# Half-array projection of 24 pairs' queries, routing kept in a PSUM bank, the next expert's sums on GpSimd, and new orders

## The chip, the cores and the metric

The kernel runs on one core of one Trainium2 chip. The core has a matrix engine (TensorE, called PE in the profile; its weight loads are the row PEld), three elementwise engines (VectorE = DVE, ScalarE = ACT, GpSimd = POOL), DMA queues (one of them issued by SyncE, called SP), an on-chip memory SBUF with 128 partitions, and PSUM, which here is one tile `ps` of eight banks of 128 x 512 float32 into which PE writes its products. Each engine works through its own list of instructions in order; semaphores hold an instruction until what it needs is there.

The metric is the device time of one execution in microseconds, the median over runs. Before the change it is 1009.02 us (1009.04, 1009.02 and 1008.69).

## What is computed

A linear attention with a feature map, whose output feeds a mixture of eight experts with a Sinkhorn routing:

```python
# q, k, v: (8, 8, 576, 64); w_phi: (64, 128)
def phi(x):
    proj = np.einsum('bhsd,df->bhsf', x, w_phi)
    proj = proj - np.max(np.abs(proj), axis=-1, keepdims=True)
    return np.concatenate([np.exp(proj), np.exp(-proj)], axis=-1)
q_p, k_p = (phi(q), phi(k))
kv = np.einsum('bhsf,bhsd->bhfd', k_p, v)
z = np.sum(k_p, axis=2)
num = np.einsum('bhsf,bhfd->bhsd', q_p, kv)
den = np.einsum('bhsf,bhf->bhs', q_p, z)[..., None] + 1e-06
x = (num / den).transpose(0, 2, 1, 3).reshape(4608, 512)

# w_gate: (512, 8); w1: (8, 512, 1024); w2: (8, 1024, 512)
logits = x @ w_gate
P = np.exp(logits - logits.max())
for _ in range(8):
    P /= P.sum(1, keepdims=True) + 1e-09
    P /= P.sum(0, keepdims=True) + 1e-09
    P *= N / E
for e in range(E):
    out += P[:, e:e + 1] * (np.maximum(x @ w1[e], 0.0) @ w2[e])
```

## The kernel before

**How the work is written down.** The program does not issue instructions directly. Each step calls `pe`, `act`, `dve`, `pool` or `dma`, which hand an operation with its reads, writes and buffers to a `Plan`. The plan sorts all of them into one order with its own estimates of durations: of the operations that could start first it takes the one written earliest, and with it the PSUM banks and buffers that this needs. So the place of a step in the text is a wish, and the lists on the engines come from the plan. Its estimates are not used as times here.

**Attention.** The 8 batches x 8 heads are 32 pairs of heads. A pair's row number is `NP * b + pr` (4 pairs to a batch), so rows 8 to 31 are the batches 2 to 7. The order of the steps is a string `order`, one letter a step, each letter taking its next pair: `a` projects a pair's k to features (tokens on the partitions), `q` projects its q in the same way to find each token's largest absolute score, `p` projects q once more with features on the partitions and takes the exponentials, `b` multiplies the k features with v, `n` and `m` multiply the q features with that for the two heads, `c` transposes the result into `xT` (the mixture's input, kept in SBUF), `r` and `g` treat the 64 tokens over and the gate, and `u` and `d` are pieces of expert 0, which needs no routing: an up piece (8 products of 512 columns and two evictions on ACT) or a down piece (8 products of 512 columns and one eviction, on ACT for odd `ts`, on DVE for even ones). The 24 `u` and 20 `d` in the string are filler for PE.

**The projection of q.** A pair's q lies transposed in `qkT`, head 0 on partitions 0 to 63 and head 1 on 64 to 127. `wphi2` holds the weights twice on a diagonal of zeros, so that a product over all 128 partitions keeps the heads apart. `tokens` (line 632) runs 4 products of 256 columns for step `q`, and `feature_rows` (line 651) 2 products of 512 columns for step `p`. Half of every such product is multiplied with zeros. Each step takes two PSUM banks: `q` gives its two back after the two maxima on DVE (line 614), `p` after the four exponentials on ACT (line 618).

**Between attention and expert 1.** After the last gate, `routing` (line 1146) runs eight rounds on DVE over `L` (128 x 36 x 8, float32): a product with the columns' factors, the row sums, their reciprocal, a product with them, the column sums over a transposed view, two subtractions that split the sums into three bfloat16 parts, one product on PE with `colw` (all ones) that adds them over the partitions, a reduction and a reciprocal. In the meantime PE runs the rest of expert 0 (`fill`, 12 up pieces and 16 down pieces). The operation `swap` (its key is `late`) gives the attention's memory to the experts' tiles when the attention's last reader is done; behind it POOL's queue loads expert 1's weights into `wx`.

**Experts 1 to 7.** The products of an expert are made with a seven-product scheme on quarters: `sums_x` and `sums_up` (lines 1434 and 1242) form sums and differences of quarters of `xT` and of `w1`, each through `sub` (line 1236), all on DVE; the first products of expert 1 (`up7`, line 1481 of the helper `wide`) need those of the first two groups of tokens and of `w1`. `sums_up` of expert 1 also waits for the routing's result `P`. From expert 2 on some of the products are split once more (`up49`, line 1613). Down products run on line 1472 and are added to the output in `acc` by DVE (line 1866) or by ACT and POOL (lines 1878 and 1881). The order of the up and down products of a unit of work is written in the table `UNITS`, one row a unit.

Of the kernel before, what the change touches and what calls it, by code (L numbers as in the profile page):

```python
# [349 lines left out]
def kernel(  # L350
# [22 lines left out]
    NG = 9  # L373
# [15 lines left out]
    colw = const.tile([128, 128], BF16, name="colw")  # L389
# [13 lines left out]
    wphi2f = wphi2.rearrange("p a b -> p (a b)")  # L403

# [31 lines left out]
    TI, GR, KM, QM, PM, NM, RM = 0, 0, 0, 0, 0, 0, 0  # L436
# [59 lines left out]
    ring("s_p", [128, NT], FP32, "rr", 1)  # L496
    ring("s_p", [128, 3, E], FP32, "cs", 1)
    ring("s_p", [128, E], FP32, "c_bc", 1)
# [243 lines left out]
    def pair_a(b, pr, t):  # L742

        h0 = (2 * pr) % 4
        s = {}
# [264 lines left out]
    def down0(g, part):  # L1010
# [5 lines left out]
        for i, ts in enumerate(tss):  # L1016
            if ts % 2:
# [37 lines left out]
    dve(128, lambda: nc.vector.memset(colw, 1.0), w=["colw"])  # L1055
# [34 lines left out]
    def stage_g(b):  # L1090
# [12 lines left out]
        "lraeaepqbwlqaqawwabwmqlltnrbppnwqbppmrmanbqaqmwwacmpnpbccpwbtcnmqnaqbclupunm"  # L1103
        "taumquglcapalbcpnqqdcenmucugbblnapmrcqdutabnqpmunpbambccddnqplanmqmducpblttb"
        "augnaqlnrbdcampcadmqeutunqcppmdcaqtdqabpbbmlrqtdnpmuaqualbnagnacctbmqulupran"
        "tdpmtdqcmdnpdabdancpcabbqmpumqbcdgnappqunburqcbugmmnqdcdanumupqbnucmcpnmbddp"
        "bqmpncncubncmmgccg"
# [34 lines left out]
    def table(buf):  # L1142

        return buf().bitcast(FP32)[:, 0:NT * E].rearrange("p (a b) -> p a b", a=NT)

    def routing():
        c_bc = None
        for it in range(8):
            rr, wv, cs, pc = new("rr"), new("T"), new("cs"), new("PP")
            lk = [("L", g) for g in range(NG)]  # L1150
            if c_bc is None:
                def u():
                    return L
                uk = lk
            else:
                ub = new("T")
                uk = [ub]

                def u(ub=ub):
                    return table(ub)  # L1160
                dve(366, lambda u=u, c=c_bc: nc.vector.tensor_tensor(
                    out=u(), in0=L, in1=c()[:, None, :].to_broadcast([128, NT, E]),
                    op=ALU.mult), lk + [c_bc], uk, shared=True)
# [901 lines left out]
```

## Time and profile before

| What | Value |
|---|---|
| median of the runs | 1009.02 us |
| span of the profiled execution, first to last instruction | 1007.1 us |
| PE busy, PEld busy | 993.4 us, 728.2 us |
| DVE, ACT, POOL busy | 897.1 us, 813.2 us, 447.0 us |
| attention, by the last transposition on PE | 0 to 203 us |
| routing on DVE | 205 to 242 us |
| first product of expert 1 | 244.2 us |
| granted TensorE clock | 1.000 of full speed |

The page of the profile gives for the profiled execution its span alone; the runs' median lies 1.9 us above it. A PE product is shown with its length through the pipeline, and products overlap, so that a busy PE need not be one at its peak; how fast PE can issue is read from long runs of equal products without a gap. A row of the view by groups reads: line, engine, operation, out<-in, shape, count | busy us, mean ns of one | idle us of the engine before them and what ended it.

### The profile page before, as it was taken

How to read it: one execution, taken by the hardware profiler on the slowest of the kernel's cores; microseconds unless marked ns; L12 is line 12 of the kernel's file. 1: busy time of each engine (PE TensorE's matmuls, PEld its weight loads, DVE VectorE, ACT ScalarE, POOL GpSimd, SP SyncE). 2: the span in 40 equal slices, each digit the busy share in tenths (PEclk: the TensorE clock that was granted, in tenths of full speed). 3: DMA queues.
4: the chain of work that ended last, by engine and by line, in shares of the span. 5: the costliest groups of instructions: out<-in, count | busy, mean ns of one | idle time of the engine just before them, and what ended most of it. 6: DMA issues, size and time to landing. Idle time of an engine off the chain costs nothing.

```text
span 1007.1 us, 23304 instructions
## 1 busy us (share of the span) xinstructions
PE 993.4 (99%) x8376; PEld 728.2 (72%) x8376; DVE 897.1 (89%) x1999; ACT 813.2 (81%) x1930; POOL 447.0 (44%) x514
## 2 busy tenths in 40 slices
PE   7899999999999999999999999999999999999998
PEld 5666666644566877777777877787778777787775
DVE  7999998987898898899989898989889988989886
ACT  7999999835979788878878788778887888778884
POOL 5778674400133344434444444444443444344443
PEclk9999999999999999999999999999999999999999
DMA  9999999181136423282327133632246222724653
GB/s 253 190 194 171 166 152 145 38 170 56 53 119 148 145 97 98 84 186 96 112 97 166 46 100 127 135 127 99 97 119 176 97 98 84 148 79 143 206 177 126
DMA packets 129748, 128.86 MB, mean 128 GB/s; under 512 B 55776, under 2 KB 98272, under 8 KB 129632
## 3 DMA queue, kind: packets, MB, share of 16 engines
q1 hardware_dynamic: 97680, 103.33, 35.5%
q0 software_dynamic: 31648, 23.86, 17.4%
q8 instruction: 65, 1.06, 0.4%
q14 instruction: 51, 0.42, 0.1%
q10 hardware_dynamic: 304, 0.20, 0.1%
HBM read 122.50 MB, written 19.53 MB: 141 GB/s over the span
## 4 chain that ended last, share of the span: by engine, by line
PE 92%; ACT 3%; DVE 2%; DMA 2%; issue 1%; POOL 0%; SPq 0%; DVEq 0%
PE ps L1472 42%; PE ps L1481 21%; PE ps L622 15%; PE ps L1613 11%; PE ps L905 2%; DMA xp<-xT 1%; ACT k L618 1%; ACT q L618 1%; DMA xi<-X 1%; PE ps L752 0%; DVE m L614 0%; ACT wx L618 0%; DVE wx L614 0%; DMA acc<-in_k_dram 0%; PE ps L934 0%
## 5 line engine op out<-in xcount | busy, mean ns | idle before, releaser
L1881 POOL TENSOR_TENSOR acc<-acc,hx 128x512 f32<-128x512 f32 x186 | 235.1, 1271 | 403.4 <-ACT hx L1878 138.5
L1472 PEld LDWEIGHTS <-hs 128*128 128x128 bf16 x1984 | 194.1, 98 | 46.6 <-issue 0.2
L1878 ACT ACTIVATE hx<-ps,P 128x256 f32<-128x256 f32 x372 | 159.3, 484 | 53.3 <-PE ps L1472 51.9
L1866 DVE SCALAR_TENSOR_TENSOR acc<-ps,P,acc 128x256 f32<-128x256 f32 x372 | 162.0, 477 | 29.8 <-PE ps L1472 28.1
L1481 PE MATMUL ps<-xT,T 128*128 128x512 bf16 x608 | 170.7, 379 | 0.0
L1472 PEld LDWEIGHTS <-hx 128*128 128x128 bf16 x1488 | 145.6, 98 | 25.1
L1472 PE MATMUL ps<-hx,hs 128*128 128x256 bf16 x992 | 144.3, 273 | 0.0
L1682 DVE CUSTOM_DVE_ANT_0 hs<-ps,U 128x512 bf16<-128x512 f32 x192 | 124.7, 684 | 10.9 <-PE ps L1481 6.6
L1613 PE MATMUL ps<-xT 128*128 128x256 bf16 x576 | 125.4, 272 | 0.0
L1481 PEld LDWEIGHTS <-T 128*128 128x128 bf16 x672 | 65.7, 98 | 40.4
L1688 ACT ACTIVATE hs<-ps 128x512 bf16<-128x512 f32 x96 | 55.8, 598 | 41.1 <-PE ps L1481 39.7
L1472 PE MATMUL ps<-wx,hs 128*128 128x256 bf16 x560 | 78.5, 273 | 0.0
L622 PE MATMUL ps<-w,hx 128*128 128x512 bf16 x288 | 73.0, 379 | 0.0
L622 PE MATMUL ps<-xT,w 128*128 128x512 bf16 x288 | 72.9, 379 | 0.0
L1472 PE MATMUL ps<-wx,hx 128*128 128x256 bf16 x496 | 72.6, 273 | 0.0
L1682 DVE CUSTOM_DVE_ANT_0 hs<-ps,X 128x512 bf16<-128x512 f32 x96 | 65.1, 683 | 7.4 <-PE ps L1613 6.6
L1472 PE MATMUL ps<-hx 128*128 128x256 bf16 x496 | 71.2, 273 | 0.0
L1613 PEld LDWEIGHTS <-xT 128*128 128x128 bf16 x576 | 56.3, 98 | 17.4
L614 DVE TENSOR_REDUCE m<-ps 128x4 f32<-128x512 f32 x88 | 58.8, 680 | 4.2 <-PE ps L622 2.0
L1472 PE MATMUL ps<-w,hx 128*128 128x256 bf16 x432 | 62.2, 273 | 0.0
L1678 ACT COPY X<-ps 128x512 f32<-128x512 f32 x96 | 58.6, 611 | 2.5 <-DVE ps L1656 2.4
L1472 PE MATMUL ps<-w,hs 128*128 128x256 bf16 x432 | 60.2, 273 | 0.0
(174 smaller groups left out, 2256.4 us busy)
## 6 DMA issues: line engine op xcount, KB each, us to landing
xT<-xi SPq DMA_DIRECT2D x48, 448.0 KB, 4.3
xT<-xd SPq DMA_DIRECT2D x72, 256.0 KB, 3.9
wx<-in_moe_w_dram POOLq DMA_DIRECT2D x8, 1024.0 KB, 11.0
v_m<-in_v_dram SPq DMA_DIRECT2D x15, 512.0 KB, 5.0
out_dram<-acc SPq DMA_DIRECT2D x14, 512.0 KB, 2.9
w<-in_moe_w_dram POOLq DMA_DIRECT2D x6, 1024.0 KB, 11.0
xT<-xp SPq DMA_DIRECT2D x24, 256.0 KB, 2.7
qk<-in_k_dram POOLq DMA_DIRECT2D x12, 256.0 KB, 5.2
```

The costliest lines, as they stand in the source:

```text
L614: dve(el, lambda: nc.vector.tensor_reduce(out=dst(), in_=src(), axis=AX.X, op=ALU.max, apply_absolute_value=True), r, w)
L618: act(el, lambda: nc.scalar.activation(out=dst(), in_=src(), func=ACT.Exp, bias=0.0, scale=scale), r, w)
L622: nc.tensor.matmul(out_, lhsT=lhsT, rhs=rhs, start=start, stop=stop)
L1472: pe(256, lambda i=i, k=k, z=z: nc.tensor.matmul(bank()[:, 256 * i:256 * i + 256], lhsT=lhs(k, i), rhs=rhs(k), start=first and z, stop=k = ...
L1481: pe(512, lambda k=k: nc.tensor.matmul(bank().rearrange("p (a b) -> p a b", a=2), lhsT=lhs(k), rhs=rhs(k), start=first and k == 0, stop=k ...
L1613: pe(256, lambda: nc.tensor.matmul(halves_of(bank[q], n)(), lhsT=lhs(), rhs=t()[:, rhs, :], start=start, stop=True, skip_group_check=True) ...
L1678: act(512, lambda: nc.scalar.copy(out=flat(to[q])(), in_=bank[q]()), [bank[q]], [(to[q], 0), (to[q], 1)])
L1682: dve(515, lambda: nc.vector._custom_dve(ADD_SAT, out=out_(q, i, j), in0=bank[q]().rearrange("p (a b) -> p a b", a=2), in1=to[q](), s0=3.0 ...
L1688: act(512, lambda: nc.scalar.activation(out=out_(q, i, j), in_=bank[q]().rearrange("p (a b) -> p a b", a=2), func=ACT.Relu, bias=0.0, scal ...
L1866: dve(320, lambda n=n, ts=ts: nc.vector.scalar_tensor_tensor(out=acc[g][:, ts, 256 * j:256 * j + 256], in0=bank()[:, 256 * n:256 * n + 256 ...
L1878: act(370, lambda n=n: nc.scalar.activation(out=u()[:, n, :], in_=bank()[:, 256 * n:256 * n + 256], func=ACT.Copy, bias=0.0, scale=P[:, 4 ...
L1881: pool(695, lambda: nc.gpsimd.tensor_tensor(out=acc[g][:, 2 * i:2 * i + 2, 256 * j:256 * j + 256], in0=acc[g][:, 2 * i:2 * i + 2, 256 * j: ...
```

## The change

It has five parts.

1. For rows 8 to 31, steps `q` and `p` of a pair no longer use `wphi2`. One block on PE runs 8 products of 128 columns over 64 partitions each (head 0 on the upper half of the array's rows, head 1 on the lower half, in turn), and right behind them the 2 products of 512 columns that step `p` used to run, again one on each half. The block takes four PSUM banks at once; step `p` is left with its exponentials. Weights without zeros (`wphi`) are made once at the start.
2. The routing's table lives in one PSUM bank. `L` is copied once in turned order by GpSimd (`Lt`), so that the column sums run over contiguous elements; the column sums are added over the partitions by a float32 product with ones, and the two subtractions and the last reduction go.
3. The sums for expert 1 (`sums_up` and the first `sums_x`, with its finer sums) are made on GpSimd instead of DVE: 8 operations of 1024 elements and 12 of 256. `sums_up` of expert 1 does not wait for `P` any more.
4. The down pieces of expert 0 for the groups 5 and 6 are evicted by ACT for even `ts` too (4 copies that were on DVE).
5. The string `order` is another behind its first 70 letters (with the same number of each letter), and the first nine rows of `UNITS` are another order of the same names.

```diff
-    TI, GR, KM, QM, PM, NM, RM = 0, 0, 0, 0, 0, 0, 0
+    TI, KM, QM, PM, NM, RM = 0, 0, 0, 0, 0, 0
+    ROWS = range(8, 32)
...
-        if not TI and not GR:
+        if not TI:
...
     def pair_a(b, pr, t):
         h0 = (2 * pr) % 4
-        s = {}
+        s, GR = {}, NP * b + pr in ROWS
...
         def maxima():
             pq = two(QM)
             if GR:
                 pts[0] = two(PM)
                 def rows():
                     for c in range(4):
                         for x in range(2):
                             half = slice(64 * x, 64 * x + 64)
                             nc.tensor.matmul(pq[1][x]()[:, 128 * c:128 * c + 128],
                                              lhsT=qkT(0, c, 1)[half], rhs=wphi[half],
                                              start=True, stop=True)
                     for x in range(2):
                         half = slice(64 * x, 64 * x + 64)
                         nc.tensor.matmul(pts[0][1][x]()[:, 0:512], lhsT=wphi[half],
                                          rhs=qkT(0, 0, 4)[half], start=True, stop=True)
...
         for i, ts in enumerate(tss):
-            if ts % 2:
+            if ts % 2 or g in (5, 6):
...
+    pool(128, lambda: nc.gpsimd.tensor_copy(out=wphi, in_=wphi_f), ["wphi_f0", "wphi_f1"], ["wphi"])
...
     order = (
...
-        "augnaqlnrbdcampcadmqeutunqcppmdcaqtdqabpbbmlrqtdnpmuaqualbnagnacctbmqulupran"
+        "bmuaangqetcqdnauppqdbtnprpuqamlbdbbnccnmccqtuaqnalpaaummbuucpnpdtbmqlmanbdctt"
...
+        pool(366, lambda: nc.gpsimd.tensor_copy(out=Lt(), in_=L.transpose([0, 2, 1])),
+             lk + ["late"], [(side, 0)])
+        dve(128, lambda: nc.vector.memset(ones(), 1.0), ["late"], [(side, 1)])
         for it in range(8):
...
+            if it:
+                dve(366, lambda: nc.vector.tensor_tensor(
+                    out=table(), in0=L, in1=c()[:, None, :].to_broadcast([128, NT, E]),
+                    op=ALU.mult), lk, [bank])
+            dve(366, lambda src=table if it else lambda: L: nc.vector.tensor_reduce(
+                out=rr(), in_=src(), axis=AX.X, op=ALU.add), lk, [bank])
+            dve(291, lambda: nc.vector.reciprocal(out=rr(), in_=rr()), [], [bank])
+            dve(366, lambda: nc.vector.tensor_tensor(
+                out=turned(), in0=Lt(), in1=rr()[:, None, :].to_broadcast([128, E, NT]),
+                op=ALU.mult), [(side, 0)], [bank])
+            dve(366, lambda: nc.vector.tensor_reduce(
+                out=cs()[:, 0], in_=turned(), axis=AX.X, op=ALU.add), [bank], [cs])
+            pe(240, lambda: mm(sums(), ones(), cs()[:, 0], True, True), [cs, (side, 1)], [bank])
+            if it < 7:
+                dve(122, lambda: nc.vector.reciprocal(out=c(), in_=sums()), [], [bank])
...
     def sums_up(e, w1):
-        late = ["late"] + (["P"] if e == 1 else [])
+        late, eng = ["late"], pool if e == 1 else dve
...
-        sub(dve, 1024, s(2), q(*a11), q(*a21), ALU.subtract, k(a11) + k(a21) + late, [S[2]])
+        sub(eng, 1024, s(2), q(*a11), q(*a21), ALU.subtract, k(a11) + k(a21) + late, [S[2]])
...
-    def sums_x(gs, r0=()):
+    def sums_x(gs, r0=(), eng=None):
...
-        "x10 X1 x11 Y1 w10 Z1 Z2 X2 x21 x20 X3 w11 x30 x40 X4 y11 x31 w20 x41 y10 w21",
+        "X1 X2 x10 w10 x11 x20 x30 x21 w11 w21 Z1 y10 x31 Z2 X3 Y1 X4 y11 x40 x41 w20",
...
         if e == 1:
-            nextX = sums_x(pairs[0])
+            nextX = sums_x(pairs[0], eng=pool)
```

The lists of the engines show the parts as follows. First PE, in attention, where the first changed pair's q is projected (row 8; `qkT` is its transposed q, `kr` and `vrd` belong to the leftover tokens of an earlier pair). Before:

```order
L622 LDWEIGHTS qkT
L622 MATMUL ps<-wphi_90,qkT 128x256
L622 LDWEIGHTS wphi_90
L622 MATMUL ps<-qkT,wphi_90 128x512
L622 LDWEIGHTS wphi_90
L622 MATMUL ps<-qkT,wphi_90 128x512
L622 LDWEIGHTS kr_527
L622 MATMUL ps<-vrd_92,kr_527 128x130
```

And of the changed kernel:

```order
L829 LDWEIGHTS qkT
L829 MATMUL ps<-wphi,qkT 128x128
L834 LDWEIGHTS wphi
L834 MATMUL ps<-qkT,wphi 128x512
L834 LDWEIGHTS wphi
L834 MATMUL ps<-qkT,wphi 128x512
L621 LDWEIGHTS kr_527
L621 MATMUL ps<-vrd_92,kr_527 128x130
```

The products of 256 columns (four of them, the last is shown) have become eight of 128 columns, and the two of 512 columns stand in the same block behind them for every one of the 24 pairs; there are 24 such blocks, each with products over all 128 rows ahead of it and behind it.

Second POOL, at the end of attention, from the loads of expert 1's weights on (`wx`), up to the first addition of an expert's output to `acc`. Before:

```order
L870 COPY r<-r_r 128x2
L517 DMA wx<-in_moe_w_dram 128x4x1024
L517 DMA wx<-in_moe_w_dram 128x8x512
L1881 TENSOR_TENSOR acc_78<-acc_78,hx 128x2x256 x3
L1881 TENSOR_TENSOR acc_79<-acc_79,hx 128x2x256 x3
```

And of the changed kernel (`X` and `xT` are the sums of `xT`, `T` and `wx` those of `w1`):

```order
L516 DMA wx<-in_moe_w_dram 128x8x512
L1244 TENSOR_TENSOR X<-xT 128x1024
L1172 COPY T<-L 128x288
L1244 TENSOR_TENSOR xT<-xT 128x2x2x256
L1244 TENSOR_TENSOR X<-xT 128x1024
L1244 TENSOR_TENSOR X<-xT 128x256
L1244 TENSOR_TENSOR X<-xT,X 128x1024
L1244 TENSOR_TENSOR T<-wx 128x1024
L1244 TENSOR_TENSOR X<-xT 128x256
L1244 TENSOR_TENSOR wx<-wx 128x2x512
L1244 TENSOR_TENSOR X<-xT,X 128x256
L1244 TENSOR_TENSOR T<-wx 128x1024
```

POOL was empty there and now holds 20 sums and the turned copy of `L`, all behind the two weight loads. Between the last gate and the first product of expert 1 PE's list had 182 products of 512 columns of expert 0, and now has 142.

Third DVE, one round of the routing. Before (`c_bc` the columns' factors, `rr` the rows'; `acc_3936` is an eviction of expert 0):

```order
L1185 TENSOR_REDUCE c_bc<-ps 128x8
L1188 RECIPROCAL c_bc<-c_bc 128x8
L1161 TENSOR_TENSOR T<-L,c_bc 128x288
L1164 TENSOR_REDUCE rr<-T 128x36
L1025 COPY acc_3936<-ps 128x512
L1166 RECIPROCAL rr<-rr 128x36
L1167 TENSOR_TENSOR T<-L,rr 128x288
L1170 TENSOR_REDUCE cs<-T 128x8
```

And of the changed kernel:

```order
L1190 RECIPROCAL ps<-ps 128x8
L1177 TENSOR_TENSOR ps<-L,ps 128x288
L1180 TENSOR_REDUCE ps<-ps 128x36
L1182 RECIPROCAL ps<-ps 128x36
L1183 TENSOR_TENSOR ps<-T,ps 128x288
L1186 TENSOR_REDUCE cs<-ps 128x8
```

Through all eight rounds DVE's list now holds the routing alone; the sums and the evictions that stood between its steps are on POOL and ACT or come later.

More of the change, by code (lines that the diff above doesn't have):

```diff
@@ new lines, in routing, with words, Lt, ones @@
+        lk = [("L", g) for g in range(NG)]
+        side, bank, cs = new("T"), new("PP"), new("cs")
+        def words(n, m):
+            return side().bitcast(FP32)[:, n:n + m]
+        def Lt():
+            return words(0, NT * E).rearrange("p (b a) -> p b a", a=NT)
+        def ones():
+            return words(NT * E, 128)
+        def table():
+            return bank()[:, 0:NT * E].rearrange("p (a b) -> p a b", a=NT)
+        def turned():
+            return bank()[:, 0:NT * E].rearrange("p (b a) -> p b a", a=NT)
```

96 lines of the change are left out of this document (32 added, 64 removed), and 48 rows, old and new, of the table UNITS.

## The prediction

> **What bounds the kernel now.** I read the page's busy times first, then the chain of waits by stage, then long runs of equal products in that chain, to see whether PE works at its peak or only looks busy.
>
> ```profile
> PE 993.4 (99%) x8376; PEld 728.2 (72%) x8376; DVE 897.1 (89%) x1999; ACT 813.2 (81%) x1930; POOL 447.0 (44%) x514
> ```
>
> PE is busy for all but 13.7 of 1007.1 us. The view by stretches (columns: length, busy time and instructions of PE, PEld, DVE, ACT, POOL, clock, DMA, GB/s) says where the rest is:
>
> ```profile
> 0.00:50.00 50.00, 41.00 (x418) 28.93 (x419) 44.43 (x93) 44.70 (x112) 32.75 (x61) 1.00 1.12 221
> 50.00:200.00 150.00, 149.29 (x1782) 98.67 (x1780) 138.40 (x324) 143.32 (x351) 99.76 (x158) 1.00 0.98 146
> 200.00:245.00 45.00, 44.92 (x258) 21.08 (x255) 38.69 (x111) 18.36 (x33) 1.73 (x2) 1.00 0.47 102
> 245.00:1007.00 762.00, 758.23 (x5926) 579.51 (x5924) 675.58 (x1475) 606.78 (x1438) 312.76 (x294) 1.00 0.41 120
> ```
>
> Nine of the idle microseconds lie in the first 50, which the change leaves as they are (its order begins with the same 70 letters, and its first changed pair is row 8). From 50 us on PE never waits for long. The chain of waits of the experts' stretch (250 us to the end) is PE alone, and the pieces of the chain give the price of a product:
>
> ```profile
> by line: PE ps L1472 55.8%; PE ps L1481 27.6%; PE ps L1613 14.6%; PE ps L622 1.6%; DVE acc L1780 0.1%; issue 0.0%
> ...
> 330.47 17.03 PE ps L1472 x156
> ```
> ```profile
> 201.28 0.22 PE ps L934 x4
> ...
> 244.34 4.32 PE ps L1481 x20
> ```
>
> 156 products of 256 columns in 17.03 us are 0.109 us each, 20 of 512 columns in 4.32 us are 0.216, and 4 of 128 columns in 0.22 us are 0.055: time in proportion to columns, without gaps. So behind 50 us a column taken from PE is time taken from the kernel, as long as something else is there for PE to do. In the attention (50 to 200 us) the two engines that evict are nearly as full: ACT 143.32 of 150, DVE 138.40. Between 200 and 245 us the routing runs on DVE, and PE covers it wholly with expert 0:
>
> ```profile
> L622 PE MATMUL ps<-w,hx 128*128 128x512 bf16 x103 | 24.0, 379 | 0.0
> L622 PE MATMUL ps<-xT,w 128*128 128x512 bf16 x82 | 19.1, 379 | 0.0
> ```
>
> (groups between 203 and 245 us: 185 products x 0.216 = 40 us, no idle time.)
>
> **The change part by part.** *The projection.* A pair's q costs 4 x 0.109 + 2 x 0.216 = 0.868 us of PE now. The new block has 8 products of 128 columns and 2 of 512, half of them on each half of the array. If the halves run side by side it takes 4 x 0.055 + 0.216 = 0.436; if they run one after another, 8 x 0.055 + 2 x 0.216 = 0.872. No product in the trace uses half the rows (every one is 128*128), so both are bounds: a gain of 24 x 0.432 = 10.4 us, or nothing. I take the first: the two products of a couple read other partitions, other weights and write other banks, nothing in the program ties one to the other.
>
> *Changing from whole to half array and back*, 48 times. The trace has no such change. At best it costs nothing; at worst PE empties its pipeline each time, and what that exposes is a product's length beyond its slot:
>
> ```profile
> L1472 PE MATMUL ps<-hx,hs 128*128 128x256 bf16 x992 | 144.3, 273 | 0.0
> ```
>
> 273 - 109 = 164 ns, so 0 to 48 x 0.164 = 7.9 us. I take the middle, 0.08 each, +3.9 us, since part of the emptying should pass under the next weight loads (PEld has 28% free). [...]
>
> *Four banks at once.* Step q took two PSUM banks and step p two more, later; the block takes four of eight before it starts, and everything in PE's list stands behind it: expert 0's filler, the next pair's k, the products with v. Today these steps hardly wait:
>
> ```profile
> L622 PE MATMUL ps<-wphi,qkT 128*128 128x256 bf16 x256 | 41.2, 276 | 1.7 <-ACT qkT L760 0.5 <-ACT wx L618 0.3 <-DVE m L614 0.3
> L622 PE MATMUL ps<-qkT,wphi 128*128 128x512 bf16 x64 | 20.5, 386 | 0.7 <-DVE m L614 0.3 <-DVE wx L614 0.2 <-DVE wx L892 0.2
> L618 ACT ACTIVATE q<-ps 128x512 bf16<-128x512 f32 x88 | 49.5, 687 | 0.2 <-PE ps L622 0.2
> ```
>
> 2.4 us of idle time in all. A block that has to wait for one more eviction waits at most about one exponential, 0.687 us: 0 to 24 x 0.687 = 16.5 us. The measured waits are far nearer to nothing; I take 0.08 a block, 1.9 us, which is nearly a doubling of those 2.4 us.
>
> *Routing and sums.* One round now takes 3.78 us (from 230.89 to 234.67), eight and the end 36.5 us (205.13 to 241.6):
>
> ```profile
> 230.89 0.67 DVE L1170 TENSOR_REDUCE cs<-T 128x8 f32<-128x288 f32 x1
> ...
> 234.67 0.68 DVE L1170 TENSOR_REDUCE cs<-T 128x8 f32<-128x288 f32 x1
> ```
> ```profile
> L1164 DVE TENSOR_REDUCE rr<-T 128x36 f32<-128x288 f32 x7 | 3.2, 453 | 0.2
> ...
> L1179 DVE TENSOR_TENSOR cs<-cs 128x8 f32<-128x8 f32 x16 | 2.6, 164 | 0.4
> ...
> L1185 DVE TENSOR_REDUCE c_bc<-ps 128x8 f32<-128x24 f32 x8 | 1.4, 180 | 2.3 <-PE ps L622 1.8 <-ACT hx L983 0.4
> ```
>
> Without the two subtractions (a pair takes 0.37 as printed, two of 164 ns) and the reduction (0.18), and with contiguous column sums at the row sums' 0.453 instead of 0.67, a round is about 3.0 us, the whole about 25. None of it is gained: PE was covered before. What it buys is that fewer products must be kept back as cover (142 after the last gate, 142 x 0.216 = 30.7 us). Under that cover POOL must finish what expert 1's first products read. The trace has no bfloat16 sums on POOL; the nearest rows are
>
> ```profile
> L810 POOL TENSOR_TENSOR v<-v_m,em 128x1024 bf16<-128x1024 f32 x22 | 42.1, 1915 | 7.4 <-ACT em L618 7.2
> L1649 POOL TENSOR_TENSOR X<-X,xT 128x256 f32<-128x256 f32 x48 | 35.2, 734 | 52.6 <-DVE hx L1240 35.1 <-ACT U L1678 9.5 <-ACT X L1678 8.0
> L517 POOL DMA_DIRECT2D wx<-in_moe_w_dram x2 | 1.7, 864 | 7.2 <-PE ps L622 7.2
> L1881 POOL TENSOR_TENSOR acc<-acc,hx 128x512 f32<-128x512 f32 x186 | 235.1, 1271 | 403.4 <-ACT hx L1878 138.5 <-DVE hx L1240 75.2 <-DVE hs L1240 62.3
> ```
>
> Two weight loads 1.7, eight sums of 1024 at 1.915 = 15.3, the turned copy and the four small sums listed among them 5 x 0.734 = 3.7: 20.7 us, under 30.7. At the dearest row (1271 ns for 512, so 2.54 for 1024) it is 25.7, still under. Cost 0. Where the cover failed, each microsecond beyond 30.7 would be PE's.
>
> The float32 product with ones replaces a bfloat16 one, eight times, in PE's list. The float32 products of the trace are longer (317 against 177 ns): bounds 0 and 8 x 0.14 = 1.1; I take 0.6.
>
> ```profile
> L752 PE MATMUL ps<-identf,acc 128*128 128x128 f32 x64 | 10.8, 317 | 4.4 <-DMA acc<-in_k_dram 3.8 <-ACT kr L618 0.3 <-DVE xb L919 0.2
> L622 PE MATMUL ps<-cs,colw 128*128 128x24 bf16 x8 | 1.4, 177 | 0.1
> ```
>
> *Four evictions to ACT*, and the new orders. ACT has 26.6 of 45 us free between 200 and 245, where most of groups 5 and 6 run, so four copies cost nothing. The orders move work whose engine count stays the same; I book them at 0, with the fuller attention among the rivals.
>
> Sum: -10.4 + 3.9 + 1.9 + 0.6 = -4.0 us; the span goes from 1007.1 to 1003.1. The runs' median lies 1.9 us above the span before, and I keep that: **1005.0 us**.
>
> **The rivals.**
>
> [...]
>
> *ACT becomes the bound of the attention.* The stretch from 50 to 200 us would shrink by about 6.5 us (10.4 less the changes of mode) to 143.5, and ACT is shown busy for 143.3 of it. Then the saved PE time turns into idle time, and the kernel stays at about 1008.5. Against: the busy share counts each instruction's tail, which the next one overlaps. The chain has three exponentials in 1.57 us, 0.52 each, not 0.687:
>
> ```profile
> 24.76 1.57 ACT k L618 x3
> ```
>
> *The four banks come late.* PE waits at the block for an eviction that DVE or ACT has not reached, and all behind it waits too. Beyond 0.08 + 4.0/24 = 0.25 us a block the change loses. At 0.42, which is some six tenths of an exponential, the time is 1005.0 + 24 x 0.34 = 1013. For it: evicting engines at over 90% in that stretch. Against: the 2.4 us of waits today.
>
> *The halves do not run side by side:* the change doesn't do what it says. 10.4 us are not gained, the rest is paid: 1015.4.
>
> *POOL's sums come late.* If they cost half as much again as the dearest row (3.8 us for 1024), the list is 8 x 3.8 + 5.4 = 35.8 us, 5 beyond the cover: 1010. [...]
>
> **How the numbers follow.** Forecast 0.56; full emptying 0.11; ACT as bound 0.12; late banks 0.10; halves in turn 0.06; late sums 0.05. The best end of all bounds is 1009.0 - 10.4 = 998.6, which needs free changes of mode and no wait; I leave it just out and begin at 999.5. Upwards the range takes in the mode changes, ACT's bound, the late sums and half of the late banks: 1012. Outside are about 0.03 below and 0.12 above. A measurement of this kernel tells 0.2%, some 2 us, from no change. Faster (under 1007.0) is nearly all of the forecast (0.52) and a third or more of the two rivals near 1009 (0.10): 0.62. Slower (over 1011.0) is the late banks, the halves in turn, half the late sums and some of the rivals' scatter: 0.22. The same: 0.16.
>
> **What would show it.** The blocks on PE: couples of 128-column products starting every 0.055 us (side by side) or 0.11 (in turn), and the two of 512 starting together or 0.216 apart. [...] PE's idle time in front of the blocks: about 2 us in all, released by ACT or DVE evictions; over 6 us is the rival of the banks. PE without a gap from the last gate to expert 1's first product, and POOL's last sum that this reads some 20 us behind the weight loads. The routing some 25 us long. Expert 1's stretch and the ones behind it as long as before. The prediction is wrong if PE idles more than 4 us more between 50 and 245 us, or if the blocks last nearer to 0.87 us than to 0.44.

## The result, and the profile after

The change makes the kernel slower: 1014.70 us (median of 5 runs, 1011.46 to 1017.63) against 1008.79 us for the kernel before on the same chip, ratio 1.0058 [1.0038, 1.0078]. A second set of runs (experiment e5) gave 1015.37 us and 1.0065 [1.0052, 1.0078]. The forecast was 1005.0 us. The runs also spread more than those of before, and most of this goes with the granted clock: the shortest, 1011.46, had a mean clock of 1.000, the longest, 1017.63, one of 0.995, and half a per cent of 1011 us is 5 of the 6.2 us between them.

The profiled execution has a span of 1011.0 us at a clock of 0.998. The view by stretches of the kernel after, cut at its own stages (columns: length, busy time and instructions of PE, PEld, DVE, ACT, POOL, clock, DMA, GB/s):

```profile
50.00:100.00 50.00, 46.97 (x620) 30.63 (x628) 46.95 (x115) 46.45 (x117) 36.91 (x58) 1.00 1.11 178
100.00:150.00 50.00, 47.96 (x565) 29.04 (x574) 42.95 (x97) 47.51 (x117) 34.01 (x55) 1.00 1.09 156
...
170.00:175.00 5.00, 3.94 (x38) 2.58 (x39) 2.90 (x9) 1.94 (x7) 2.40 (x4) 0.66 0.59 144
...
208.00:244.00 36.00, 35.37 (x206) 17.69 (x209) 21.99 (x55) 16.95 (x31) 26.79 (x23) 1.00 0.58 127
244.00:1011.00 767.00, 762.65 (x5943) 581.39 (x5945) 676.71 (x1476) 606.45 (x1439) 312.33 (x294) 1.00 0.41 119
```

In the attention, where before PE was idle for 0.7 of 150 us, it is now idle for 3.0 and 2.0 us of the first two rows (40 of 8480 products are missing from this trace, so a little of that is no idle time), and around 172 us it runs at 0.66 of its clock. The first product of expert 1 starts at 242.7 us, 1.5 us earlier than before. But 23 of expert 0's products, which stood ahead of it, now come behind it (23 x 0.216 = 5.0 us), and the blocks take 5.5 us less of PE (below): some 10 us less work, and 1.5 us gained. What PE waited for between 50 and 260 us (us in total, times, longest):

```profile
PE ps L621 <- DMA rT<-qk_r: 2.5, 2, 1.4
PE ps L621 <- DMA xT<-wx: 1.3, 1, 1.3
PE ps L621 <- DVE cs L1186: 0.4, 1, 0.4
PE ps L621 <- issue: 0.4, 2, 0.2
PE ps L621 <- DVE m L613: 0.3, 1, 0.3
```

In the same stretch of the kernel before PE waited for no transfer; the view has two waits there:

```profile
PE ps L622 <- ACT wx L618: 0.3, 1, 0.3
PE ps L622 <- DVE m L614: 0.3, 1, 0.3
```

The first two lines of the kernel after are transpositions by DMA: of the tokens left over (`rT`, step `r`) and of a pair's result (`xT`, step `c`). PE asks for them earlier than before. On PE's timeline of the kernel before, the products with `rT` near 102 and 138 us follow transfers that had landed 9.5 and 2.8 us earlier:

```profile
101.68 0.60 PE L622 MATMUL ps<-wphi,rT 128*128 128x256 bf16 x4
...
138.28 0.60 PE L622 MATMUL ps<-wphi,rT 128*128 128x256 bf16 x4
```

On that of the kernel after they start the moment the transfer lands (in brackets: idle time ahead, and what ended it):

```profile
95.33 0.39 PE L621 MATMUL ps<-wphi,rT 128*128 128x256 bf16 x2 [1.39 <-DMA rT<-qk_r]
...
137.68 0.61 PE L621 MATMUL ps<-wphi,rT 128*128 128x256 bf16 x4 [1.08 <-DMA rT<-qk_r]
```

With the new string and less work ahead, PE reaches the first of these readers 6.4 us earlier than before. The transfer itself ends 3.5 us later (at 95.7 and not at 92.2 us), because the load that it turns came in at 88.7 us and not at 85.0, as the chain of waits of the kernel after has it (start, length, what):

```profile
81.40 7.25 DMA qk_r<-in_q_dram
88.72 6.57 DMA rT<-qk_r
```

The room that the lists had is used up. The third wait stands at 170 us, in front of a filler product of expert 0, and what comes behind it runs at half speed:

```profile
169.37 0.19 PE L904 MATMUL ps<-kv,qr 128*128 128x65 bf16 x1
170.84 0.38 PE L621 MATMUL ps<-xT,w 128*128 128x512 bf16 x1 [1.28 <-DMA xT<-wx]
...
171.77 0.62 PE L621 MATMUL ps<-w,hx 128*128 128x512 bf16 x1
...
174.30 0.74 PE L621 MATMUL ps<-w,hx 128*128 128x512 bf16 x2
...
175.47 0.60 PE L621 MATMUL ps<-w,hx 128*128 128x512 bf16 x2
```

A product of 512 columns shows 0.62 us there in place of 0.38, for 3.4 us (171.2 to 174.6).

The blocks themselves do what they should. One of them, on PE's timeline:

```profile
164.70 0.38 PE L621 MATMUL ps<-xT,w 128*128 128x512 bf16 x1
165.02 0.40 PE L829 MATMUL ps<-wphi,qkT 64*128 64x128 bf16 x8
165.25 0.38 PE L834 MATMUL ps<-qkT,wphi 64*128 64x512 bf16 x2
165.56 0.39 PE L621 MATMUL ps<-xT,w 128*128 128x512 bf16 x1
```

From the start of the first of the eight small products to that of the two long ones are 0.23 us, four couples of 0.055, not eight products of it; from there to the next whole-array product 0.31, one long slot of 0.216 and a gap. So the halves run side by side, and a block takes 0.64 us with both changes of the array, against 0.868 before: 24 x 0.228 = 5.5 us less work for PE. No block waits for banks.

The routing and the sums of expert 1 (groups of DVE between 205 and 245 us; of POOL between 200 and 245 us):

```profile
L1183 DVE TENSOR_TENSOR ps<-T,ps 128x288 f32<-128x288 f32 x8 | 3.7, 462 | 2.7 <-POOL T L1172 2.5
L1186 DVE TENSOR_REDUCE cs<-ps 128x8 f32<-128x288 f32 x8 | 3.7, 457 | 0.3
```
```profile
L1244 POOL TENSOR_TENSOR X<-xT 128x256 bf16<-128x256 bf16 (+1 forms) x8 | 8.2, 1035 | 2.3 <-DMA xi<-X 2.2
...
L1244 POOL TENSOR_TENSOR T<-wx 128x1024 bf16<-128x1024 bf16 x2 | 4.2, 2112 | 0.0
```

A column sum over contiguous elements takes 0.457 us, a sum of 1024 elements on POOL 2.11 (the line with 1035 ns mixes sums of 1024 and of 256). Expert 1 waits for neither.

### The profile page after: what moved, and what is told of

The parts are those of the page before. It is cut to its first block, busy times and chain, and to the rows that moved or that the text cites. A ratio compares the mean times of both kernels' runs of the same rounds, so it can differ in the third digit from the quotient of the medians.

```text
span 1011.0 us, 23416 instructions
## 1 busy us (share of the span) xinstructions
PE 989.0 (98%) x8440; PEld 720.8 (71%) x8480; DVE 883.2 (87%) x1951; ACT 814.5 (81%) x1934; POOL 470.8 (47%) x536
## 4 chain that ended last, share of the span: by engine, by line
PE 88%; DVE 3%; ACT 3%; DMA 3%; POOL 1%; issue 1%; SPq 0%; POOLq 0%; DVEq 0%; ACTq 0%
PE ps L1476 42%; PE ps L1485 21%; PE ps L621 12%; PE ps L1617 11%; PE ps L904 1%; ACT q L617 1%; DVE m L613 1%; DMA rT<-qk_r 1%; ACT k L617 1%; DMA qk_r<-in_q_dram 1%; DMA xT<-wx 1%; DMA acc<-in_q_dram 1%; PE ps L829 1%; DVE ps L912 0%; DVE wx L613 0%
## 5 line engine op out<-in xcount | busy, mean ns | idle before, releaser
L1485 PE MATMUL ps<-xT,T 128*128 128x512 bf16 x608 | 171.2, 379 | 0.0
L621 PE MATMUL ps<-w,hx 128*128 128x512 bf16 x270 | 70.7, 382 | 0.8 <-issue 0.2
```

Of the source, the lines that this page charges most:

```text
L621: nc.tensor.matmul(out_, lhsT=lhsT, rhs=rhs, start=start, stop=stop)
L1485: pe(512, lambda k=k: nc.tensor.matmul(bank().rearrange("p (a b) -> p a b", a=2), lhsT=lhs(k), rhs=rhs(k), start=first and k == 0, stop=k ...
```

## The experiments

All ratios below are against the kernel before, run on the same chip in turn with the experiment.

**One part alone, one part undone.** e1 is the kernel before with the blocks alone:

```diff
-        s = {}
+        s, GR = {}, NP * b + pr in ROWS
...
+            pts[1], pts[0] = two(QM), two(PM)
...
+            o = plan.op("PE", 4 * 0.056 + 0.222, 0.22, rows, [(t["T"], 0, h0 // 2), "wphi"],
+                        pq[0] + pts[0][0])
```

> The kernel before with the half-array blocks for rows 8 to 31 alone; routing, sums and both orders as before (where step p stands ahead of step q, the block runs at p). Each block saves 0.868 - 0.641 = 0.23 us of PE by the trace of the changed kernel, 5.5 us in all. Theory A (the new attention order makes DMA transpositions late, and PE waits for them): without that order no such wait, 1003 to 1005 us, spread under 1 us. Rival B (any kernel with less PE work in attention meets the limit of ACT and DVE, so the saved time turns to idle time): 1008 to 1010. Rival C (the four banks of a block come late when the order is not made for it): 1010 or more, with idle time of PE in front of the blocks.

e2 is the change without the blocks:

```diff
-    ROWS = range(8, 32)
+    ROWS = range(0)
```

> The changed kernel without the half-array blocks (no row uses them), its new orders, routing and sums kept. Theory A: the late transpositions stay, or shrink a little because PE is slower: 1014 to 1020 us, with waits of PE for DMA on rT or xT. Rival B: with the old projection the attention is as dense as before, so 1008 to 1010 and no waits. Rival D (routing in PSUM and sums on GpSimd cost time themselves): above 1010, with idle time of PE between 200 and 250 us, not before.

e3 is the change with the string `order` and the table `UNITS` of before, e4 the kernel before with those of the change:

```diff
-        "lraeaepqbwlqaqawwabwmqlltnrbppnwqbppmrmanbqaqmwwacmpnpbccpwbtcnmqnaqbcunnclpt"
+        "lraeaepqbwlqaqawwabwmqlltnrbppnwqbppmrmanbqaqmwwacmpnpbccpwbtcnmqnaqbclupunm"
...
```

> The changed kernel with the order string and the table of units of before; half-array blocks, routing and sums as changed (where step p stands ahead of step q, the block runs at p). Theory A: 1003 to 1005 us and runs within 1 us of one another. Rival B: 1008 to 1010. Rival D: slower than the kernel with the blocks alone by more than 2 us.

> The kernel before with the order string and the table of units of the change, and nothing else. Theory A: the order alone brings the waits of PE for transpositions: 1012 to 1018 us, and runs that differ by several us. Rival B: 1008 to 1010, since PE has its old work.

Measured: e1 1016.11 us, 1.0078 [1.0059, 1.0097]; e2 1051.25 us, 1.0419 [1.0398, 1.0440]; e3 1028.29 us, 1.0189 [1.0171, 1.0207]; e4 1059.31 us, 1.0501 [1.0480, 1.0521]. The times of theory A and of rival B missed in all four. Those of the rivals C (e1) and D (e2, e3) came true, but not by their causes: in e1 no block waited for its banks (PE's longest wait in attention was 2.0 us, for `xT<-wx`); in e2 PE idles from 50 us on, not only behind 200; in e3 expert 1 starts at 245.0 us, 9 us earlier than in e1, so that what e3 loses against e1 lies behind the routing. A string that meets a kernel it was not searched for gives 8 to 51 us more than before, more than any part of the change is worth, so that nothing about the single parts can be read from these four. They say one thing: the order and the kernel go together, so that the order was not a part to be booked at zero. Here is e2 from 210 to 220 us, and what PE waited for most between 50 and 250 us:

```profile
210.00:220.00 10.00, 7.76 (x89) 5.74 (x86) 9.51 (x24) 7.58 (x19) 2.94 (x7) 0.58 0.16 36
```
```profile
PE ps L621 <- DMA qkT<-qk: 2.9, 1, 2.9
PE ps L621 <- POOL r L869: 2.4, 1, 2.4
PE ps L904 <- DVE ps L912: 1.7, 5, 0.7
```

PE idles at many places, and the clock falls there too: by stretches of 50 us it is 0.97, 0.93 and 0.90 from 100 to 250 us, and in this stretch it is 0.58. From here on the lists of the change are kept as they are, and single entries of them are edited.

**The change once more, its loads earlier, its blocks wide.** e5 is the change again:

> The changed kernel itself once more, beside the two that follow on the same chip: all theories expect 1011 to 1018 us. It is the reference for them.

e6 issues the loads for the tokens left over earlier on POOL's queue, all else in its place:

```diff
+    EARLY = {4: [5, 5, 5, 5], 6: [1, 3, 3, 3]}
...
+        for o in [o for o in done if o.early]:
+            i = done.index(o)
+            same = [k for k in range(i) if done[k].eng == o.eng]
+            done.insert(same[-o.early], done.pop(i))
```

> The changed kernel; on GpSimd's queue alone the loads of the leftover tokens of batches 4, 5 and of 6, 7 are issued 5 and 1 to 3 places earlier, 3 to 5 us sooner, so that their transpositions rT should land before PE asks. The lists of PE, DVE, ACT and of SP's queue are the same. Theory A2 (the lists are made on estimates of when a transfer lands; where it lands later PE, which works in order, stands): the two waits for rT (1.4 and 1.1 us) go and 2 to 4 us with them. Rival B (PE waits there for the evicting engines anyway, the transfers only come last): under 1 us.

e7 keeps every list and runs the blocks over all 128 rows with the zero-padded weights, as before the change (it computes the same):

```diff
-                                             lhsT=qkT(0, c, 1)[half], rhs=wphi[half],
+                                             lhsT=qkT(0, c, 1), rhs=wphi2[:, x, :],
...
-                        nc.tensor.matmul(pts[0][1][x]()[:, 0:512], lhsT=wphi[half],
-                                         rhs=qkT(0, 0, 4)[half], start=True, stop=True)
+                        nc.tensor.matmul(pts[0][1][x]()[:, 0:512], lhsT=wphi2[:, x, :],
+                                         rhs=qkT(0, 0, 4), start=True, stop=True)
```

> The changed kernel with its lists unchanged, instruction for instruction, but the products of the 24 blocks run over all 128 rows, with the weights padded with zeros; nothing runs side by side and the array is never switched. A block takes 0.872 instead of 0.641 us. If PE's time in the attention is what the kernel's time is made of (theory A2, and the step of the prediction): 5 to 6 us more than the changed kernel. Rival B (the saved time ends up as waits for ACT and DVE): the same as the changed kernel within 2 us.

Measured: e5 1015.37 us, span 1010.0 in its profile. e6 1014.49 us, 1.0061 [1.0041, 1.0080], its twelve runs from 1008.90 to 1019.42, its profile with a span of 1007.1 us and a clock of 1.000. e7 1014.59 us, 1.0063 [1.0044, 1.0082], its profile 1013.9. So wide blocks, with 5.5 us more work for PE, cost next to nothing in the median of these lists, as rival B of e7 had it; its profile alone is longer than that of e5, by 3.9 us. And with PE's old work on q these lists are 6.1 us over before: the loss is in the lists and needs no saving on PE. The waits of PE in e6 between 50 and 260 us:

```profile
PE ps L912 <- ACT acc L1025: 1.9, 1, 1.9
PE ps L629 <- DVE cs L1194: 0.4, 1, 0.4
```

The waits for `rT` are gone in this execution, and so is the one for `xT`, whose transfer was not moved. A new wait came with this, at 76 us, since the four loads now stand on POOL ahead of a small operation that ACT's exponentials need. The profile gained 3 us on e5, as theory A2 had it, the median 0.9, as rival B had it: only three of the twelve runs had a clock of 1.000 (1008.90, 1009.97 and 1011.56 us), the other nine lay between 1013.57 and 1019.42 at 0.995 to 0.998. The mean clock does not account for all of that spread: 1013.85 and 1018.75 both had 0.998.

**Early loads with wide blocks (e8), two more transfers moved (e9).** e8 is the edits of e6 and e7 together.

> The early loads of e6_early_loads and the blocks over all rows of e7_full_blocks in one kernel, every list the same as in both; it computes the same. PE has 24 x 0.23 = 5.5 us more work than in e6. Theory 'transfers' (the saving of the blocks is swallowed where the next thing PE needs is a transfer that comes late anyway): with the late transfers gone PE is the bound of the attention, so the wide blocks must cost nearly their whole price here, a profile span of about 1007.1 + 5 = 1012, with under 2 us of waits for transfers between 100 and 250 us. Theory 'evictors' (ACT and DVE set the pace of the attention, PE's share does not matter): the span stays within 1.5 us of e6's, 1007 to 1008.5. On the clock: if it falls because PE has idle spots, the fuller PE keeps it at 0.999 to 1.000 in most runs and they lie within 4 us of one another; if it falls for another reason, they spread over 8 us or more as in e6.

e9 goes on from e6:

```diff
-    EARLY = {4: [5, 5, 5, 5], 6: [1, 3, 3, 3]}
+    EARLY = {4: [5, 5, 1, 1], 6: [1, 3, 3, 3]}
...
+    def stage_t(n):
+        turn_qk(halves[2 + n // 2, n % 2])
+        plan.ops[-1].early = -(n == 10)
```

> The kernel of e6 with two more moves among the transfers, every other list the same; it computes the same. On POOL's queue only two of the four loads for the tokens left over of batches 4 and 5 are issued ahead of the small operation on the maxima that an ACT exponential waits for (in e6 all four were, and PE then waited 1.9 us for ACT at 70 us). On SP's queue the transposition xT<-wx near 164 us, for which PE waits in after, e5, e7 and e8 (1.3 to 2.1 us), is issued ahead of a transposition of q and k instead of behind it. Theory: the change's loss is made of a few late transfers and of the clock that falls in some executions after the wait at 164 to 175 us. Then the profile shows no wait of PE over 1 us between 50 and 250 us, the first product of expert 1 starts at 238 to 240 us, the span is 1004.5 to 1006.5, and the runs keep a clock of 0.999 or 1.000 and lie within 4 us of one another: median 1006 to 1008.5, level with before or under it. Rival: the clock falls for other reasons (shorter products on half the array, less work for PE): then the profile improves in the same way, but the runs spread over 8 us or more at clocks of 0.995 to 1.000, and the median stays at 1011 or above.

Measured: e8 1017.21 us, 1.0077 [1.0058, 1.0096], six runs from 1012.35 to 1019.56, four of them at 0.998; e9 1016.71 us, 1.0076 [1.0059, 1.0093], 1013.15 to 1018.32. Both spans that were named for e8, 1012 and 1007 to 1008.5, were missed: it is 1017.2. The expectation for the clock failed too: with a fuller PE it fell in four runs of six. The profile shows what happened in one execution, in the three longest waits between 50 and 260 us and in two stretches:

```profile
PE ps L629 <- DMA xT<-wx: 2.1, 1, 2.1
PE ps L912 <- ACT acc L1025: 1.6, 1, 1.6
PE ps L629 <- POOL wx L823: 1.1, 1, 1.1
```
```profile
170.00:175.00 5.00, 3.84 (x72) 3.00 (x71) 4.12 (x9) 5.00 (x16) 2.76 (x6) 1.00 1.49 173
175.00:180.00 5.00, 4.01 (x39) 2.53 (x39) 2.50 (x8) 1.05 (x5) 2.40 (x4) 0.66 1.09 193
```

It has e6's lists, and the same transposition that came in time in e6's profile came 2.1 us late here; behind it the clock fell once more, to 0.66 in the second stretch. That PE had 5.5 us more work in sum did not keep this from happening behind one hole of 2.1 us. In e9 the wait for `xT<-wx` is gone, as meant, but the theory's other numbers missed:

```profile
PE ps L629 <- DMA rT<-qk_r: 4.3, 2, 3.0
PE ps L629 <- DVE m L621: 1.7, 2, 1.4
```

The longest wait, 3.0 us at 138 us, is for a transposition whose last load was issued 1.4 us later than in e6 and landed 5.2 us later (at 134.2 us, not at 129.0); why it took so much longer is not shown. The rival of e9 held in its median, 1011 or above, but not in the rest: the profile did not improve, and the runs spread over 5 us where it had 8 or more. Moving transfers by hand moved the waits about.

**Lists with room (e10, e11).** The planner reckons landings later, and the string was searched anew for it:

```diff
                 o.end = landed[0] + 1.0
+                if landed[0] < 198:
+                    o.end += 1.25 if o.turn else 1.5 if o.eng == "POOL" else 0.0
...
-        "lraeaepqbwlqaqawwabwmqlltnrbppnwqbppmrmanbqaqmwwacmpnpbccpwbtcnmqnaqbcunnclpt"
+        "lraeaepqbwlqaqawwabwmqlltnrbppnwqbppmrmanbqaqmwwacltpbnmwaamcqpb"
...
```

> The changed kernel with every part of the change in it, but with lists that leave room for late transfers: the planner reckons the landing of the attention's transpositions 1.25 us later and of GpSimd's loads 1.5 us later than in the change, and the string that orders the steps was searched anew for that planner. It computes the same. The spans less PE's waits between 50 and 250 us are 1004.8 in after, 1004.5 in e5, 1003.7 in e6 and 1005.2 in e9, against 1006.3 in before: that is what the change should be worth if nothing came late. Theory (the parts of the change are worth about what was forecast, and its new order, which has transfers landing just in time, gives it back in waits and in falls of the clock behind them): PE waits less than 1.5 us for transfers between 50 and 250 us, the span is 1004 to 1007, the clock 0.999 or 1.000 in most runs, median 1006 to 1009, at least 3 us under the change and level with before or under it. Rival (with the blocks the attention is bound by something that any order runs into, evictors or transfers): the waits between 50 and 250 us stay over 4 us in other places, the span is 1009 or more and the median 1011 or more.

> The same as e10 with a second string from the same search and 1.25 us for both kinds of transfers; it computes the same. It is there to tell the luck of one string from the room for transfers. Theory: as e10, span 1004 to 1007, median 1006 to 1009, clock 0.999 or 1.000 in most runs. If the result hangs on the single string and not on the room, the two kernels differ by more than 4 us. Rival: median 1011 or more, as for e10.

Measured: e10 1012.50 us (1011.63 to 1014.91), 1.0044 [1.0032, 1.0057]; e11 1011.11 us (1010.47 to 1014.02), 1.0036 [1.0023, 1.0050]. The two agree within 1.4 us, lie 2 to 4 us under the change, and nine of their ten runs have a clock of 0.999 or 1.000. That is half of the theory. The other half, a time level with before, missed, and the numbers of the rival came true: in both a median of 1011 or more and waits of over 4 us, in e10 a span of over 1009 too (e11 has 1008.7). Each still has a wait for one transposition, and some for other engines. e10, then e11:

```profile
PE ps L623 <- DMA qkT<-qk: 1.9, 1, 1.9
PE ps L623 <- POOL v L817: 1.8, 2, 1.5
```
```profile
PE ps L623 <- DMA xT<-wx: 1.6, 1, 1.6
PE ps L623 <- DVE m L615: 0.9, 2, 0.5
```

**The waits taken away (e12).** The lists and the transfers are those of the change, entry for entry; some products read a tile that is there already.

```diff
-        tokens(pp, lambda c: rT()[:, c, :], NP, [rT], own)
+        tokens(pp, lambda c: W[0][0]()[:, c, 0:128] if b >= 4 else rT()[:, c, :], NP, [rT], own)
...
-                           rT().rearrange("p a b -> p (a b)"), True, True),
+                           W[0][0]()[:, 0, 0:512] if b >= 4 else
+                           rT().rearrange("p a b -> p (a b)"), True, True),
...
+                        xT[:, dc, 0:512] if w and 3 <= g <= 6 else
                         xT[:, dc, g * 512:(g + 1) * 512], dc == 0, dc == NP - 1),
```

> The changed kernel with every list and every transfer as in the change; only what some products of PE read is another. The projections of the tokens left over of batches 4 to 7 read a weight tile in place of the turned rT, and the up products of expert 0 for the groups 3 to 6 read the columns of group 0 in place of their own, so that PE waits for no transposition rT<-qk_r and none xT<-wx or xT<-xb there (those tokens' and groups' part of the output is not computed). Theory (the work of the change is worth 1 to 3 us, and its lists give this back at those two kinds of transfers and in the falls of the clock behind them): PE waits under 2 us between 50 and 250 us, the first product of expert 1 starts at 238 to 241 us, the span is 1004.5 to 1006.5, the clock 0.999 or 1.000 in nearly every run, the runs lie within 4 us and their median is 1006 to 1009, 6 us or more under the change. Rival (evictors or other transfers take the place of those waits at once): waits of 4 us or more between 50 and 250 us, the span 1009 or more, the median 1011 or more. On the clock: if it falls without such waits too, the runs still spread over 6 us or more at clocks down to 0.996.

Measured: 1008.39 us (11 runs, 1007.34 to 1010.17), before 1008.54, ratio 1.0000 [0.9991, 1.0009]; the span is 1006.6 us, the first product of expert 1 starts at 238.3 us, and nine of the eleven runs have a clock of 0.999 or 1.000. The waits and the stretches:

```profile
PE ps L621 <- POOL wx L816: 0.9, 1, 0.9
PE ps L621 <- DVE cs L1188: 0.4, 1, 0.4
PE ps L621 <- DVE m L613: 0.3, 1, 0.3
```
```profile
100.00:150.00 50.00, 49.08 (x571) 29.80 (x581) 43.42 (x98) 48.63 (x119) 34.96 (x58) 1.00 1.12 170
150.00:175.00 25.00, 24.51 (x301) 14.85 (x306) 21.91 (x51) 23.92 (x60) 14.51 (x24) 1.00 0.98 159
175.00:203.00 28.00, 27.73 (x384) 17.42 (x389) 26.30 (x65) 26.90 (x64) 11.89 (x20) 1.00 0.14 35
```

This settles the larger part. The change's median lies 6.3 us above this one (1014.70 - 1008.39; over before, 5.9 and 6.8 us in the change's two sets of runs, -0.2 here), and what differs is that PE reads two kinds of turned tiles as soon as they can be there, with the falls of the clock behind such waits. The profiled executions differ by 4.4 us: there are 3.1 us less of waits (table below), and the change's 3.4 us at half clock are another 1.7. Of the theory of e12 the start of expert 1, the clock, the spread of 2.8 us and the median held; the span missed by 0.1 us, and the waits, 3.1 us, are over the 2 that were expected. The rivals fall: no wait for an evictor or another transfer is longer than 0.9 us. What is left of the change without these waits is level with before, not faster.

A last view over all profiled executions: the span, PE's waits over 0.06 us between 50 and 260 us (summed over its products), and the one less the other.

| Kernel | span | waits | clock | span less waits |
|---|---|---|---|---|
| before | 1007.1 | 0.8 | 1.000 | 1006.3 |
| the change | 1011.0 | 6.2 | 0.998 | 1004.8 |
| e5, the change again | 1010.0 | 5.5 | 1.000 | 1004.5 |
| e6, early loads | 1007.1 | 3.4 | 1.000 | 1003.7 |
| e9, transfers moved | 1013.8 | 8.6 | 1.000 | 1005.2 |
| e10, room in the plan | 1010.6 | 5.6 | 1.000 | 1005.0 |
| e11, room in the plan | 1008.7 | 4.9 | 0.999 | 1003.8 |
| e12, no late reads | 1006.6 | 3.1 | 1.000 | 1003.5 |
| e7, wide blocks | 1013.9 | 5.0 | 1.000 | 1008.9 |
| e8, wide blocks, early loads | 1017.2 | 6.6 | 0.998 | 1010.6 |

With the waits taken out, the changed kernels lie at 1003.5 to 1005.2, 1.1 to 2.8 us under before, and those with wide blocks 4 to 7 us above them. The same comes out of the starts of PE's products, in the traces that hold all of them. At the slot that each form takes in a run without gaps, the products add up to 984.8 us of work in before, 980.5 in e5, 980.2 in e6 and 985.8 in e7: the change takes 4.3 to 4.6 us from PE, and the wide blocks give 5.3 back. What PE loses between 50 and 260 us beyond these slots is 2.2 us in before, 8.9 in e5, 6.7 in e6 and 7.4 in e7. That is 1.4, 3.4, 3.3 and 2.4 us more than the waits of the table, which begin only when the shown length of the product ahead has ended. So the blocks' saving is there, and the lists give it back as lost time. This rests on one execution of each kernel. In the medians e7 is no longer than the change. It did lose less to the clock (four of its six runs at 1.000, three of ten of the change), but at 1.000 too its runs have a median of 1013.1 us against 1011.8, so that most of the 5.5 us does not show there. The lists without late reads were not run with wide blocks, which would have told.

## Why the prediction was wrong

The forecast was -4.0 us, and +5.9 were measured. By its own steps:

*The projection.* Right in the mechanism and nearly in size. The halves run side by side; the block's own time is 0.45 us where 0.436 was worked out.

*The changes of the array.* 0.094 us each (0.095 going in, 0.092 coming out, from the spacing of the products around the blocks) where 0.08 was taken: 4.5 us, not 3.9. That is little more than half of the 0.164 that a product's whole tail would be. The full emptying, with 0.11 among the chances, falls.

*Four banks.* No block waited for its banks. The 1.9 us booked here were about what other small waits came to (e12 has 3.1 us of waits, before 0.8), but those are ahead of other steps, released by POOL, DVE and ACT.

*The float32 product* takes 0.14 us of PE's list where the bfloat16 one took 0.03 (from the starts of its neighbours): 0.9 us in all, 0.6 booked.

*Routing and sums.* The round takes 3.16 us (3.0 forecast), the routing 27.7 us, of which 2.5 are its wait for the turned copy on POOL; POOL's last sum that expert 1 reads first ended at 231.3 us, 11 us ahead of its use. Covered, as said.

*"The orders move work whose engine count stays the same; I book them at 0."* This is the step that failed. The count of work is the same, but the string also decides how long after its issue a transfer is first read. The prediction looked at the order only for the filler that covers the routing, and did not compare, in the list of the change, the places of the `rT` and `xT` readers with those of their transfers. By e12 the two kinds of late reads cost 6.3 us, and by e7 the new lists cost 6.1 us over before even with the old work on q. The prediction's own sign of failure, over 4 us more idle time on PE between 50 and 245 us, came true (6.2 against 0.8).

*The clock* does not appear in the prediction at all. In the stretches of before that the prediction shows it stands at 1.00, with no wait of PE over 0.3 us behind 50 us; a forecast that adds waits has to add what the clock may do behind them, 1.7 us in the profiled execution of the change.

*Late banks* fall: no block waits. *ACT as the bound* is not shown: what e12 leaves of the change is level with before, as that rival's 1008.5 had it, but its waits are short ones with many releasers, and ACT is a small part of them. *Halves in turn* and *late sums* fall by the rows above.

Of the 9.9 us between forecast and result, the late reads and the clock are 6.3; the blocks and the float32 product gave 4.6 us where the sum had 5.9, which is 1.3; the other waits are 2.3 us more than before where 1.9 were booked, 0.4. That adds up to 8.0. The other 1.9 us fit what the view of waits leaves out: by the starts of its products PE loses 2.0 us more beside those waits in e5, and 1.9 more in e6, than in before. For e12 itself this cannot be counted, as its trace lacks 40 products.

What stays open is whether some string keeps the 3 us without waits. e10 and e11 gained 2 to 4 us on the change and no more; no version here beats the kernel before. Why the same transposition comes late by 1.3 us in one execution and by 1.9 in another of the same kernel (the change and e5), and in time in e6, was not tried.

## What to carry to other kernels

Where a list is planned from estimates, compare for every transfer how long before its first reader it lands, before and after a change; here a reader came 6.4 us earlier and its transfer 3.5 us later, and 9.5 us of spare room became a wait of 1.4. A new order is a change of its own, and with a planner that answers to each shift it cannot be judged by counting work or by undoing one part: keep the lists and edit single entries, or let a reader take a tile that is there already, as in e12. And when the runs of a kernel begin to spread, look at its longest waits and at the clock behind them before looking for a cause in the work.

## What the hardware showed that was not expected

Behind a single wait the clock of a PE that was otherwise full fell to half in the change and in e8. A hole of 1.28 us at 170 us in the change was followed by 3.41 us at a clock of 0.50, and one of 2.1 us at 174 us in e8 by a mean clock of 0.66 from 175 to 180 us, which is what 3.4 us at half would give. Waits of 1.9 us at the same place in e5 and of 3.0 us at 138 us in e9 had no fall behind them: the clock stays at 1.00 there. The stretches of one clock that begin and end inside the trace are 163.84, 3.413 and 836.27 us long in the change, which is 48, 1 and 245 times the short one, and 996.69 us in before, 292 times. Both falls came behind a stretch with little work: in the 3.41 us ahead of its fall PE started products of 2846 columns in sum in the change, and in e8 those started in the 3.5 us up to the first slow product (172.50 to 175.99 us) have 2265. Counted in the same steps of 3.41 us, the next fewest of the change behind 50 us, beside the slow stretch itself, are 4185, at 92.7 us, and the fewest of before 6233; neither has a fall behind it. A limit is not shown: in e3 PE was busy for 3.00 of the 5 us from 175 us on, less than the 3.84 of 5 ahead of the fall in e8, and its clock stays at 1.00 there and in the stretch behind.

In the change, two products of 128 columns on the two halves of the array start 2 to 4 ns apart, and couples follow every 56 ns (66 after the first), which is the 55 ns of one such product: the second half added nothing that shows. Going from the whole array to halves and back cost 0.19 us here (0.095 and 0.092), so that of the 0.41 us that a block saved without it 0.23 were left.
